# Delta-rule attention and two feed-forward networks in one kernel: attention outputs built transposed in 32-column pieces, the second network's weights staged already split, one planner for the whole order

## Chip, cores and metric

One core of a Trainium2 chip. The metric is the device time of one execution in microseconds (us), lower is better: the median of three runs. Matmuls run on PE (weights are loaded on PEld); DVE, ACT and POOL are the three elementwise engines; SP issues all DMAs.

## What is computed

The reference, cut to what matters:

```python
for t in range(S):                      # S=768, batch 4, 8 heads, head dim 48
    y[:, :, t] = einsum(q_t, state)
    v_old = einsum(state, kn_t)         # kn = normalised k
    state = state + beta_t * outer(kn_t, v_t - v_old)
x = y, heads side by side               # 3072 tokens x 384
x = elu(x @ w_in1) @ w_out1             # d_ff 2048
h = x @ w_in2                           # d_ff 2048
out = ((a0+a1*h+a2*h2+a3*h3) / (1+|b0||h|+|b1|h2+1e-6)) @ w_out2
```

The four weight matrices are float64 on the host and reach the kernel as their int64 bits; the kernel turns them into fp32 itself.

## The kernel before, in words

**Numbers.** Every product of the two networks is made of three fp32r matmuls: high part of the weight by high part of the data, high by low, low by high. A "split" (`split`, L519) makes the high part as an ACT copy that rounds to fp32r and the low part as a subtraction on DVE or POOL. The products of the attention are plain fp32 matmuls, which the trace shows as two PE records each.

**Attention.** The 768 tokens are cut into 12 scan steps `s` of 64 tokens; two steps make a window `w` (`WINS`). `g_item` (tile `gp`) makes the Gram blocks of a step, `t_pieces` solves the triangular systems of a window on DVE, and `chain` (L848) does the sequential part of each step for two halves `hf`: `ks`, `u1`, `lo`, `u2` (tiles `ks`, `cb`), `yy` (the outputs, L934), `xx` (L957) and `ku` (the update of the state `s_bd`). `yy` makes y token by feature, 64x96 at a time: 8 matmuls on the state and 8 on the step's own updates `ub`, accumulated in one PSUM tile of 128x384. An ACT copy (DVE for step 0) brings it to SBUF, `xx` transposes it with three PE transposes, a second ACT copy puts the result into `xs`, and `split_x` (L838) splits the window's `xs` into `xh` and `xl`, one buffer each.

**First network.** For each window and each of 16 feature blocks `f`: `H` (9 matmuls, tile `h`), `A1`/`B1`/`C1` (the elu and its split, tiles `e`, `pe`, `gh`, `gl`), `wo_split` (the output weights are split anew in every window), `O` (9 matmuls into the accumulators `o`). The attention of window w+1 runs between the H and O of window w. `evac1` writes a window's result to DRAM (`x2d`); its third part goes through `tmp`, the scratch tile of `t_pieces`.

**Weights.** `conv_x`, `conv_d`, `conv_s` (L603 to L633) turn a half block of float64 bits (128x192 pairs, tile `raw`) into fp32: two ACT operations, two DVE operations, and a split or a store. Windows 1 to 4 have 8 such half blocks each: the second network's output weights `o2`, stored as fp32 in `w2d`. Its input weights `i2` (32 half blocks) are converted and split in window 5, the last, where `load_w2`/`split_w2` also read `o2` back (tile `w2r`) and split it.

**Second network.** 48 steps `k` of two feature blocks each: `H2` (18 matmuls, PSUM `h_b` for even k, `h_a` for odd), `A2`/`B2`/`C2` (the rational function), `O2` (18 matmuls). `h_a` takes the PSUM of the first network's `h` tiles, so `pair_tile` waits for their last reader.

**What sets the order.** All operations are recorded (`Recorder`), each with an event time given by `at(...)`. `order` (L309) runs a list scheduler (`simulate`, costs in `PEC`, `LEAVE`, `ENTER`, `PAIR`) six times with due times from `backward`, and the best order is emitted. That holds for operations up to event time `P + Q["tm"]`; the rest, nearly all of the second network, is emitted in event order. All instructions carry the line of the recorder's call, so the trace is read by tile names.

Of the kernel before, what the change touches and what calls it, by code (L numbers as in the profile page):

```python
# [172 lines left out]
class Recorder:  # L173
    LAT = 70

# [67 lines left out]
    def act(self, out, in_, **kw):  # L243
        n = out.ids.size
        d = 200 + n * .833 - (30 if in_.base.psum else 0)
        extra = [x for x in kw.values() if isinstance(x, View)]
        d += 90 * len(extra)
        self.add("ACT", self.nc.scalar.activation, dict(out=out, in_=in_, **kw), [out], [in_] + extra, d - 100, d)
# [6 lines left out]
    class Eng:  # L255
# [3 lines left out]
        def __getattr__(self, op):  # L259
            def call(*pos, **kw):  # L260
# [26 lines left out]
                self.rec.add(self.name, fn, kw, outs, ins, d - (80 if self.name == "DVE" else 40), d, port=port)  # L287
# [11 lines left out]
    "xx": (90, 405), "wm": (200, 500)}  # L299
LEAVE = {"F": 2040, "so": 1062, "lo": 812, "ks": 804, "gp": 914, "ku": 855, "yy": 1471, "xx": 290, "wm": 500}  # L300
ENTER = {"F": 0, "so": 71, "ks": 71, "xx": -25, "ku": 70, "yy": 20, "gp": -20, "lo": 100, "wm": 50}
PAIR = {
# [3 lines left out]
FAR = 1 << 60  # L306
# [33 lines left out]
def simulate(ops, given=None):  # L340
# [3 lines left out]
    bus = 0.0  # L344
    port = 0.0
    gleft, gready = {}, {}
    mode, size, began = None, 0, 0.0
    done = 0
    rank = {}
# [6 lines left out]
    queue = None  # L356
    if given is not None:
        queue = {e: [] for e in free}
        for o in given:
            u = o.group if o.group is not None else o  # L360
            if o.group is None or o.group.ops[0] is o:
                rank[u] = len(queue[o.eng])
                queue[o.eng].append(u)
        turn = dict.fromkeys(free, 0)

    def pri(u):
        return u.n if isinstance(u, Group) else u.late

    def push(u, r):
        e = "PE" if isinstance(u, Group) else u.eng  # L370
        k = rank[u] if rank else r
        heapq.heappush(pend[e], (k, u.ops[0].n if isinstance(u, Group) else u.n, r, u))
    for o in ops:
        if o.group is None:
            if not o.left:
                push(o, 0.0)
        elif o.group.ops[0] is o and not gleft[o.group]:
            push(o.group, 0.0)
    total = sum(1 for o in ops if o.group is None) + len(gleft)
    end = 0.0  # L380

    def finish(o, t):
        nonlocal end
        end = max(end, t)
        for s in o.succ:
            k = s.deps[o]
            if s.group is not None and s.group is o.group:
                continue
            r = o.start if k == "s" else t + (0 if o.eng == "PE" else 33 if s.eng != "POOL" or s.eng == o.eng else 75)
            if s.group is not None:  # L390
                g = s.group
# [4 lines left out]
            else:  # L396
                s.ready = max(s.ready, r)
                s.left -= 1
                if not s.left:
                    push(s, s.ready)  # L400
    while done < total:
        pick = None
        for e in free:
            if queue is not None:
                if not pend[e] or pend[e][0][0] != turn[e]:
                    continue
                t = max(free[e], pend[e][0][2])
            else:
                if not pend[e] and not head[e]:
                    continue  # L410
                t = free[e]
                if not head[e]:
                    t = max(t, pend[e][0][0])
            if pick is None or t < pick[0]:
                pick = t, e
        t, e = pick
        if queue is not None:
            u = heapq.heappop(pend[e])[3]
            turn[e] += 1
        else:  # L420
            while pend[e] and pend[e][0][0] <= t:
                _, n, r, u = heapq.heappop(pend[e])
                heapq.heappush(head[e], (pri(u), n, u))
            i = 0
            if e == "PE" and mode not in (None, "F"):
                small = [x for x in head[e] if x[2].kind != "F"]
                if small:
                    i = head[e].index(min(small))
            u = head[e][i][2]
            head[e].remove(head[e][i])  # L430
            heapq.heapify(head[e])
        if e == "PE":
            if mode is not None:
                t = max(t, began + pe_cost(mode, u.kind) * size)
            mode, began = u.kind, t
            size = 1.0
            if u.kind == "F":
                size = len(u.ops) / 9
            elif u.kind == "yy":
                size = len(u.ops) / 16  # L440
# [5 lines left out]
        else:  # L446
            o = u
            o.start = t
            if e == "SP":
                free[e] = t + o.pitch  # L450
                bus = max(bus, t + 300) + o.bytes / 230.0
                finish(o, max(t + o.lat, bus + 1300) + 100)
            else:
                d = 0.0
                if o.port:
                    w = max(0.0, port - t - 135)
                    if w > 0:
                        d = w
                    port = t + d + o.lat
                free[e] = t + d + o.pitch  # L460
                finish(o, t + d + o.lat)
# [995 lines left out]
```

## Time and profile before

| | us |
|---|---|
| median of 3 runs | 1054.34 (1053.87 to 1055.9) |
| the profiled execution | 1053.65 |
| its span, first to last instruction | 1051.9 |
| PE busy | 986.0 |
| DVE busy | 886.6 |
| ACT busy | 752.4 |
| POOL busy | 429.6 |

The profiled execution's time holds 1.75 us beside its span, and lies 0.69 below the median. The program has three stretches: up to 95.6 us only attention runs (Gram blocks, the first solve, scan steps 0 and 1); from 95.6 to about 650 the first network runs with the attention of the next window between its matmuls; from about 650 the second network runs. A busy time of PE is no measure of its speed; how far apart equal blocks of matmuls start is.

### The profile page before, as it was taken

How to read it: one execution, taken by the hardware profiler on the slowest of the kernel's cores; microseconds unless marked ns; L12 is line 12 of the kernel's file. 1: busy time of each engine (PE TensorE's matmuls, PEld its weight loads, DVE VectorE, ACT ScalarE, POOL GpSimd, SP SyncE). 2: the span in 40 equal slices, each digit the busy share in tenths (PEclk: the TensorE clock that was granted, in tenths of full speed). 3: DMA queues.
4: the chain of work that ended last, by engine and by line, in shares of the span. 5: the costliest groups of instructions: out<-in, count | busy, mean ns of one | idle time of the engine just before them, and what ended most of it. 6: DMA issues, size and time to landing. Idle time of an engine off the chain costs nothing.

```text
span 1051.9 us, 22800 instructions
## 1 busy us (share of the span) xinstructions
PE 986.0 (94%) x9064; PEld 813.2 (77%) x9064; DVE 886.6 (84%) x1234; ACT 752.4 (72%) x1477; POOL 429.6 (41%) x351
## 2 busy tenths in 40 slices
PE   7159998999989999999999999999999999999997
PEld 6047876878878887888888887788888888888885
DVE  4988976987798588849943689999999999999997
ACT  4479879877677777666656999777667677676764
POOL 1376555544303222312322355554534545436332
PEclk9568989999999999999999998999999999999999
DMA  9656145514651652043020435101001010010000
GB/s 259 207 152 201 38 131 169 179 60 117 186 189 48 185 148 101 17 132 107 12 88 1 135 106 158 61 1 60 0 1 61 1 60 1 1 61 1 31 1 30
DMA packets 51852, 91.89 MB, mean 87 GB/s; under 512 B 7073, under 2 KB 29729, under 8 KB 51745
## 3 DMA queue, kind: packets, MB, share of 16 engines
q1 hardware_dynamic: 51744, 90.43, 28.1%
q8 instruction: 71, 1.16, 0.5%
q14 instruction: 37, 0.30, 0.1%
HBM read 77.83 MB, written 12.58 MB: 86 GB/s over the span
## 4 chain that ended last, share of the span: by engine, by line
PE 68%; DVE 14%; ACT 12%; issue 3%; DMA 1%; POOL 1%; SPq 0%; ACTq 0%; DVEq 0%; POOLq 0%
PE o L193 29%; PE h L193 11%; PE h_a L193 9%; PE h_b L193 8%; DVE tmp L193 3%; PE gp L193 3%; PE y L193 3%; PE cb L193 3%; ACT wo L193 2%; ACT e L193 2%; DVE wo L193 2%; PE ku L193 1%; DVE tt L193 1%; ACT raw L193 1%; DVE gl L193 1%
## 5 line engine op out<-in xcount | busy, mean ns | idle before, releaser
L193 POOL TENSOR_TENSOR gl<-wo 128x1024 fp32r<-128x1024 f32 x47 | 146.3, 3113 | 197.1 <-DVE wo L193 157.4
L193 POOL TENSOR_TENSOR wor<-wo,wor 128x384 fp32r<-128x384 f32 x96 | 113.6, 1184 | 244.3 <-ACT wor L193 221.5
L193 PE MATMUL o<-gh,wor 128*128 128x512 f32 x576 | 198.7, 404 | 7.9 <-ACT wor L193 4.3
L193 ACT ACTIVATE wo<-wo 128x192 f32<-128x192 f32 (+3 forms) x254 | 150.5, 631 | 70.5 <-DVE wo L193 62.0
L193 PE MATMUL h<-xh,wi 128*128 128x512 f32 x546 | 183.7, 396 | 1.4 <-issue 0.6
L193 PE MATMUL o<-gh,wo 128*128 128x512 f32 x576 | 139.0, 390 | 0.1
L193 PEld LDWEIGHTS o<-gh,wor 128*128 128x128 f32 x576 | 109.7, 191 | 35.4 <-ACT wor L193 5.0
L193 PEld LDWEIGHTS o<-gh,wo 128*128 128x128 f32 x576 | 107.5, 188 | 23.8 <-ACT ys L193 0.9
L193 PEld LDWEIGHTS h<-xh,wi 128*128 128x128 f32 x546 | 102.3, 188 | 25.7 <-issue 1.1
L193 PE MATMUL o<-gl,wor 128*128 128x512 f32 x288 | 114.2, 397 | 0.0
L193 DVE SCALAR_TENSOR_TENSOR e<-e,pe 128x512 f32<-128x512 f32 x96 | 78.6, 819 | 35.4 <-ACT e L193 33.3
L193 PE MATMUL h<-xl,wi 128*128 128x512 f32 x273 | 106.7, 391 | 1.2 <-DVE tt L193 0.9
L193 DVE TENSOR_TENSOR gl<-e,gh 128x512 fp32r<-128x512 f32 x88 | 70.8, 805 | 32.1 <-ACT gh L193 31.9
L193 PE MATMUL h_a<-xh,wi 128*128 128x512 f32 x288 | 93.9, 394 | 2.1 <-DVE wo L193 2.1
L193 PE MATMUL h_b<-xh,wi 128*128 128x512 f32 x288 | 93.2, 392 | 0.0
L193 DVE SCALAR_TENSOR_TENSOR wo<-wo 128x1024 f32<-128x1024 f32 (+2 forms) x71 | 81.8, 1157 | 7.4 <-ACT wo L193 7.3
L193 ACT ACTIVATE e<-h 128x512 f32<-128x512 f32 x91 | 54.1, 594 | 46.2 <-PE h L193 42.0
L193 ACT ACTIVATE gh<-e 128x512 fp32r<-128x512 f32 x96 | 60.3, 629 | 30.2 <-PE o L193 17.6
L193 PE MATMUL o<-gl,wo 128*128 128x512 f32 x288 | 73.5, 390 | 1.6 <-DVE gl L193 1.6
L193 DVE SCALAR_TENSOR_TENSOR gh<-wo,ab_sb 128x1024 fp32r<-128x1024 f32 (+1 forms) x49 | 65.9, 1344 | 6.4 <-ACT wo L193 0.2
L193 PEld LDWEIGHTS h_a<-xh,wi 128*128 128x128 f32 x288 | 54.8, 190 | 14.1 <-DVE wo L193 2.5
L193 PEld LDWEIGHTS o<-gl,wo 128*128 128x128 f32 x288 | 53.9, 188 | 13.6 <-DVE gl L193 2.4
(126 smaller groups left out, 2085.6 us busy)
## 6 DMA issues: line engine op xcount, KB each, us to landing
kv<-c_kv SPq DMA_DIRECT2D x24, 576.0 KB, 6.4
gin<-g_in SPq DMA_DIRECT2D x69, 192.0 KB, 3.7
kq<-c_kq SPq DMA_DIRECT2D x22, 512.0 KB, 4.4
raw<-w_out SPq DMA_DIRECT2D x42, 192.0 KB, 2.8
raw<-w_in SPq DMA_DIRECT2D x34, 192.0 KB, 2.4
wo<-w_in SPq DMA_DIRECT2D x30, 192.0 KB, 3.9
xr<-x2d SPq DMA_DIRECT2D x6, 768.0 KB, 5.5
out_t<-ys SPq DMA_DIRECT2D x18, 256.0 KB, 2.3
```

Of the source, the lines that this page charges most:

```text
L193: fn(**{k: v.real() if isinstance(v, View) else v for k, v in kw.items()})
```

## The change

1. **Attention outputs.** `yy` swaps the operands: the state and the updates are now the stationary side, cut into pieces of 32 columns, and q, k or p stream with 64 columns. The result stands feature by token in PSUM, in strips of 32 partitions that follow each other in turn: 24 matmuls of 32x64 on the state and 24 on the updates in place of 8 and 8 of 64x96. `xx`, both copies and `split_x` are gone; ACT writes `xh` straight from PSUM and DVE writes `xl` from PSUM and `xh`, 128x384 per half. `xh` and `xl` have two buffers.
2. **Second network's weights.** All 64 half blocks are converted in windows 1 to 4 (16 each), split by ACT and DVE into `cs`, and stored split in DRAM (`i2d`, `o2d`). In window 5 `load_i2` and `load_o2` bring 32 blocks of 393 KB to where they are used.
3. **One order.** The planner now orders everything, in 8 rounds, with other estimates (`gap`, 8 DMAs in flight, due times with the releasing engine's delay) and a choice that may hold an engine for a more urgent operation that comes soon (`choose`).
4. **Times.** `H2(0)` and `H2(1)` get events inside window 5, both in `h_b`. Half of the Gram blocks of a window get later events. The third part of `evac1` gets its own tile `xe`; `p` and `lo` have 3 buffers in place of 4.

The core of the diff:

```diff
-                y = pa.tile([128, DM], F32, tag="pa", name="y")
-                rc.brk("yy")
+                y = pa.tile([128, 3, 128], F32, tag="pa", name="y")
+                rc.brk("yt")
+                parts = [(d["kq"], s_bd)] if s > 0 else []
+                parts.append((p_d[s], d["ub"]))
+                seen = set()
+                for n, (r, l) in enumerate(parts):
+                    for bl in range(2):
+                        for i in range(4):
+                            u = 4 * bl + i
...
+                            lt = lt.rearrange("p a b -> p (a b)")
+                            for g in range(3):
+                                c, o = divmod(3 * i + g, 4)
+                                mm(out=y[32 * o:32 * o + 32, c, 64 * bl:64 * bl + 64], lhsT=lt[:, 32 * g:32 * g + 32], rhs=rhs,
+                                   start=o not in seen, stop=n == len(parts) - 1 and bl == 1 and c == 2)
+                                seen.add(o)
...
+                xh, xl = (t[:, :, c0:c0 + 128] for t in xt[w])
+                act(out=xh, in_=y, func=AF.Copy)
+                vector.tensor_tensor(out=xl, in0=y, in1=xh.bitcast(F32), op=ALU.subtract)
...
-    w2d = dr.tile([NF, 128, DM], F32, name="w2d")
+    w2d = {k: dr.tile([NF, 128, 2, DM], F32, name=f"{k}d") for k in ("i2", "o2")}
...
+            t = mp.tile([128, 2, HD], F32R, tag="cs", name="cs")
+            split(t, e, vector)
+            rc.dma(out=w2d[k][i, :, :, cs], in_=t.bitcast(F32))
...
+    def load_i2(f):
+        rc.dma(out=wi_tile(f).bitcast(F32), in_=w2d["i2"][f])
+
+    def load_o2(f):
         wo2[f] = p2p.tile([128, 2, DM], F32R, tag=f"wo2{f}", name=f"wo2{f}")
-        split(wo2[f], w2t.pop(f), vector)
+        rc.dma(out=wo2[f].bitcast(F32), in_=w2d["o2"][f])
...
-        at(Q["g1"] + Q["g1d"] * i, fn)
+        at(Q["g1"] + Q["g1d"] * i if i < 4 else i - 40, fn)
...
-            for f in range(8):
-                conv_at(T + 2 * f + .15, .5)
+            for f in range(NF):
+                conv_at(T + f + .15, .5)
...
-        for h in range(2):
-            conv_at(T + f + Q["c5"] + .4 * h, Q["c5d"])
-        at(T + f + Q["l5"], load_w2, f)
-        at(T + f + Q["l5"] + 1, split_w2, f)
+        at(T + f + 1.1, load_i2, f)
+        at(T + f + 1.2, load_o2, f)
...
+            at(T + (8.7, 14.4)[k], H2, k)
...
-    first, then = rc.ops[:cut], rc.ops[cut:]
-    _, first = order(first, 6)
+    _, first = order(rc.ops, 8)
```

Where it moves instructions. First PE at the end of the start, from the outputs of scan step 1 to the first matmul of the first network (`h`). Before:

```order
L193 MATMUL y<-s_bd,kq 64x96 x8
L193 MATMUL y<-ub,p 64x96 x8
L193 MATMUL y<-s_bd,kq 64x96 x8
L193 MATMUL y<-ub,p 64x96 x8
L193 MATMUL xt<-cm_sb,y_1071 128x128 x3
L193 MATMUL ku<-ub,kv 48x48 x32
L193 MATMUL xt<-cm_sb,y_1098 128x128 x3
L193 MATMUL gp<-gin 128x128 x4
L193 MATMUL ks<-s_bd,kq 32x48 x64
L193 MATMUL h_1262<-xh,wi_405 128x512
```

With the change:

```order
L191 MATMUL y<-kq,s_bd 32x64 x24
L191 MATMUL y<-p,ub 32x64 x24
L191 MATMUL y<-kq,s_bd 32x64 x24
L191 MATMUL y<-p,ub 32x64 x24
L191 MATMUL ku<-ub,kv 48x48 x32
L191 MATMUL h_1262<-xh,wi_355 128x512
```

The transposes are gone, and the Gram block and `ks` of step 2 now stand behind the first `h`. Earlier in the start, 16 of the Gram matmuls (`gp`) of window 1 moved from ahead of the first solve to between the outputs of step 0 and `ks` of step 1.

Second, DVE where the second network begins (the operations on `h_b` belong to `H2`; `wo_86` is scratch of the rational function, `raw` and `ce` belong to the conversion of weights). Before, at `H2(0)`:

```order
L193 TENSOR_TENSOR wo_86<-wo_86,h_b 128x1024
L193 SCALAR_TENSOR_TENSOR raw<-raw 128x192
L193 SCALAR_TENSOR_TENSOR raw_8480<-raw_8480 128x192
L193 SCALAR_TENSOR_TENSOR ce<-raw 128x192
L193 SCALAR_TENSOR_TENSOR ce<-raw_8480 128x192
L193 SCALAR_TENSOR_TENSOR wo_86<-wo_86,ab_sb,h_b 128x1024
L193 SCALAR_TENSOR_TENSOR e<-e,pe 128x512
L193 SCALAR_TENSOR_TENSOR raw<-raw 128x192
```

With the change:

```order
L191 TENSOR_TENSOR gl<-e,gh 128x512
L191 SCALAR_TENSOR_TENSOR e<-e,pe 128x512
L191 TENSOR_TENSOR wo_86<-wo_86,h_b 128x1024
L191 TENSOR_TENSOR gl<-e,gh 128x512
L191 SCALAR_TENSOR_TENSOR wo_86<-wo_86,ab_sb,h_b 128x1024
L191 SCALAR_TENSOR_TENSOR e<-e,pe 128x512
L191 SCALAR_TENSOR_TENSOR wo_86<-wo_86 128x1024
L191 TENSOR_TENSOR gl<-e,gh 128x512
```

No conversion is left there; only the elu of window 5 (`e`, `gl`) stands between the operations of `H2(0)`.

Third, SP's queue in window 5. Before:

```order
L193 DMA raw<-w_in 128x384
L193 DMA raw_8282<-w_in 128x384
L193 DMA raw<-w_in 128x384
L193 DMA w2r<-w2d 128x384
L193 DMA raw_8346<-w_in 128x384
```

With the change:

```order
L191 DMA wi_8736<-i2d 128x768
L191 DMA i2d<-cs 256x1x192
L191 DMA wi_8766<-i2d 128x768
L191 DMA wi_8793<-i2d 128x768
L191 DMA i2d<-cs 256x1x192
L191 DMA xr<-x2d 128x3x512
L191 DMA wo_8812<-o2d 128x768
```

Loads of finished weights stand where loads of raw bits stood; a load of `wi` waits for the last reader of the first network's block in the same place.

## Rows read from the trace of the kernel before

**Rows 1.** The page: busy time of each engine.

```profile
PE 986.0 (94%) x9064; PEld 813.2 (77%) x9064; DVE 886.6 (84%) x1234; ACT 752.4 (72%) x1477; POOL 429.6 (41%) x351
```

**Rows 2.** Stretches: us, busy PE, PEld, DVE, ACT, POOL, PEclk, DMA share, GB/s.

```profile
0.00:95.60 95.60, 52.13 (x1013) 45.60 (x1013) 74.03 (x169) 59.40 (x199) 43.79 (x63) 0.71 0.71 208
...
190.00:287.00 97.00, 96.16 (x1134) 79.27 (x1128) 79.84 (x139) 70.17 (x168) 41.70 (x37) 1.00 0.43 132
...
567.00:646.40 79.40, 79.40 (x354) 65.69 (x353) 59.45 (x98) 72.78 (x179) 39.41 (x41) 1.00 0.38 117
646.40:673.10 26.70, 21.99 (x73) 16.17 (x72) 25.88 (x34) 21.46 (x43) 13.33 (x12) 0.81 0.33 104
673.10:1032.60 359.50, 359.40 (x1585) 297.07 (x1584) 346.50 (x267) 251.03 (x252) 170.15 (x75) 1.00 0.06 20
1032.60:1051.90 19.30, 13.23 (x55) 9.67 (x53) 12.95 (x18) 7.26 (x12) 2.70 (x1) 0.96 0.11 41
```

**Rows 3.** Chain of waits, 696 to 712 us: start, us, what.

```profile
701.86 4.08 PE h_a L193 x18
```

**Rows 4.** Windows 1 to 4 as one stretch: all, then tile `raw` (DVE, ACT, POOL).

```profile
190.00:567.00 377.00, 370.68 (x4935) 305.95 (x4930) 291.29 (x517) 258.98 (x575) 108.49 (x98) 1.00 0.34 107
190.00:567.00 377.00, 32.51 (x70) 25.02 (x77) 2.33 (x4) 1.00 0.34 107
```

**Rows 5.** Timeline of PE where the second network begins: [idle before <-releaser].

```profile
651.12 0.79 PE L193 MATMUL o<-gh,wor 128*128 128x512 f32 x1 [2.55 <-ACT wor L193]
...
667.31 0.50 PE L193 MATMUL h_a<-xh,wi 128*128 128x512 f32 x1 [2.10 <-DVE wo L193]
```

**Rows 6.** Chain of waits, 84 to 97 us.

```profile
85.43 3.90 PE y L193 x64
...
89.81 1.57 PE ku L193 x64
...
95.62 1.60 PE h L193 x6
```

**Rows 7.** Instructions by tile: nanoseconds of one, min/median/max.

```profile
L193 ACT ACTIVATE xs<-xt x24: 467/490/493, 71.6 to 571.2; 128x384 f32<-128x384 f32 x24
L193 DVE TENSOR_TENSOR xl<-xs,xh x18: 673/684/1505, 93.5 to 574.6; 128x512 fp32r<-128x512 f32 x18
L193 DVE TENSOR_TENSOR R<-kv,ks x22: 509/544/554, 75.9 to 551.4; 128x384 f32<-128x384 f32 x22
L193 DVE SCALAR_TENSOR_TENSOR raw<-raw x35: 344/356/1461, 206.0 to 389.8; 128x192 int32<-128x192 int32 x35
L193 DVE TENSOR_TENSOR wo<-w2r,wo x16: 543/548/952, 596.6 to 665.1; 128x384 fp32r<-128x384 f32 x16
```

**Rows 8.** Timeline of PE in the start, scan step 1.

```profile
76.60 0.28 PE L193 MATMUL cb<-R,tp_t 32*32 32x48 f32 x2 [2.72 <-DVE tmp L193]
78.55 1.50 PE L193 MATMUL cb<-R,tp_t 32*32 32x48 f32 x62 [1.67 <-DVE R L193]
```

**Rows 9.** Timeline of PE, one scan step's outputs, 387 to 398 us.

```profile
387.81 0.88 PE L193 MATMUL y<-s_bd,kq 128*64 128x96 f32 x16
...
390.60 0.55 PE L193 MATMUL xt<-cm_sb,y 128*128 128x128 f32 x3
391.08 1.64 PE L193 MATMUL ku<-ub,kv 128*48 128x48 f32 x64
392.65 0.55 PE L193 MATMUL xt<-cm_sb,y 128*128 128x128 f32 x3
392.95 0.48 PE L193 MATMUL o<-gh,wor 128*128 128x512 f32 x1
...
395.10 1.05 PE L193 MATMUL gp<-gin 96*128 96x128 f32 x8
396.08 1.58 PE L193 MATMUL ks<-s_bd,kq 128*32 128x48 f32 x128
397.59 0.50 PE L193 MATMUL h<-xh,wi 128*128 128x512 f32 x1
```

**Rows 10.** Waits of PE, 95 to 646 us: total, times, longest us.

```profile
PE o L193 <- ACT tmp L193: 2.7, 2, 2.0
```

More of the change, by code (lines that the diff above doesn't have):

```diff
@@ L343, in simulate @@
     head = {e: [] for e in free}
[L344 to L349, printed above, removed]
+    bus = port = end = began = 0.0
+    mode, size, done = None, 1.0, 0
+    gleft, gready, landed = {}, {}, []
     for o in ops:
@@ L355, in simulate @@
             gready[o.group] = 0.0
[L356 to L367, printed above, removed]
-    def push(u, r):
[L370 to L380, printed above, removed]
+    def push(u, r):
+        if isinstance(u, Group):
+            heapq.heappush(pend["PE"], (r, u.n, u))
+        else:
+            heapq.heappush(pend[u.eng], (r, u.n, u))
     def finish(o, t):
@@ L400, in finish, with choose @@
                     push(s, s.ready)
+    def choose(e, t):
+        cand = sorted(head[e])
+        for late, n, u in cand[:6]:
+            stop = t + u.pitch
+            for r, _, c in pend[e]:
+                if r < stop and stop - c.late > max(0.0, r + c.pitch - late):
+                    break
+            else:
+                head[e].remove((late, n, u))
+                return u
+        return None
+    for o in ops:
+        if o.group is None:
+            if not o.left:
+                push(o, 0.0)
+        elif o.group.ops[0] is o and not gleft[o.group]:
+            push(o.group, 0.0)
+    total = sum(1 for o in ops if o.group is None) + len(gleft)
     while done < total:
@@ L403, in simulate @@
         for e in free:
[L404 to L415, printed above, removed]
-        t, e = pick
[L417 to L431, printed above, removed]
+            if pend[e] or head[e]:
+                t = free[e] if head[e] else max(free[e], pend[e][0][0])
+                if pick is None or t < pick[0]:
+                    pick = t, e
+        t, e = pick
+        while pend[e] and pend[e][0][0] <= t:
+            _, n, u = heapq.heappop(pend[e])
+            head[e].append((u.n if e == "PE" else u.late, n, u))
         if e == "PE":
+            small = [x for x in head[e] if x[2].kind != "F"] if mode not in (None, "F") else None
+            x = min(small or head[e])
+            head[e].remove(x)
+            u = x[2]
             if mode is not None:
@@ L435, in simulate @@
             mode, began = u.kind, t
[L436 to L440, printed above, removed]
+            size = len(u.ops) / SIZE[mode] if mode in SIZE else 1.0
             for o in u.ops:
@@ L580, in raw_tile @@
             return wo1[:, i].rearrange("p (n two) -> p n two", two=2).bitcast(I32)
-        if p2q is not None and n % 2:
-            return p2q.tile([128, HD, 2], I32, tag="raw2", name="raw2")
         return mp.tile([128, HD, 2], I32, tag="raw", name="raw")
@@ L1080, in evac1 @@
             else:
-                xs = tmp[:, 0:NC]
+                xs = ap1.tile([128, 512], F32, tag="xe", name="xe")[:, 0:NC]
             act(out=xs, in_=acc[w][c][:, 0:NC], func=AF.Copy)
@@ L1132, in A2 @@
         if k not in e2:
-            e2[k] = [w[:, 1024 * (2 * i + k % 2):1024 * (2 * i + k % 2) + 1024] for i in range(3)]
+            e2[k] = [w[:, 1024 * i:1024 * i + 1024] for i in (range(3, 6) if k % 2 else range(3))]
         sq, ab, u = (t[:, n] for t in e2[k])
@@ L1358 @@
     ev.sort(key=lambda x: x[:2])
-    cut = None
     for t, _, fn, a in ev:
-        if t >= P + Q["tm"] and cut is None:
-            cut = len(rc.ops)
         fn(*a)
-    first, then = rc.ops[:cut], rc.ops[cut:]
-    _, first = order(first, 6)
+    _, first = order(rc.ops, 8)
     nc.scalar.preload_act_table_set("natural_log_exp_and_others")
     with tc.manual_schedule():
-        for o in first + then:
+        for o in first:
             o.emit()
```

176 lines of the change are left out of this document (65 added, 111 removed), and 2 rows, old and new, of the table PAIR.

## Prediction

> **What bounds the kernel now.** I read the page's busy times first: PE is busy 94% of the span, DVE 84%, ACT 72% [rows 1]. That names PE and says nothing about where it loses time. So the second view is the table by stretch [rows 2], and beside it the chain of waits [rows 3] for how far apart equal blocks start.
>
> The second network is at its pace: 18 matmuls take 4.08 us, 227 ns each [rows 3], for 359.5 us without an idle PE [rows 2]. Nothing in the change makes these matmuls cheaper. In windows 1 to 4 PE is busy 370.7 of 377 us [rows 4], so time is won there by giving PE less to do, and a faster ACT or DVE wins nearly nothing. PE is slack in two places. In the start, to 95.6 us, it is busy 52 us, at a mean granted clock of 0.71, a mixture of its two levels, 1.2 and 2.4 GHz [rows 2]. Where the second network begins, 646.4 to 673.1 us, it does four blocks of 18 matmuls, which cost 4 x 4.08 = 16.3 us at full pace, in 26.7 us, at a clock of 0.81: 10.4 us lost [rows 2, 3]. DVE is busy 25.9 of these 26.7 us, and PE waits there once for the split of `wor` and once for DVE [rows 5]. DVE is late because it still converts the `i2` weights between the first operations of the second network.
>
> The sum is made against the profiled execution, 1053.65 us; the median of the runs is 0.69 us above it.
>
> **The start.** Before, the outputs of scan step 1 begin at 85.43 and take 3.90 us; the first `h` matmul comes at 95.62 [rows 6], 6.29 us after they end. In between PE does two sets of transposes, `ku`, a Gram block and `ks`. In the new order only `ku` (1.57 us) is left, and beneath it lies the new way to `xh` and `xl`: an ACT copy of 128x384 from PSUM (0.49 us, as `xs`) and a DVE subtraction that reads PSUM (0.54 us, as `R`) [rows 7]. So `h` starts 6.29 - 1.57 = 4.7 us earlier. Against that, 16 Gram matmuls move behind the first solve, ahead of step 1. Four of them take 0.98 us at full clock [rows 9], 16 take 3.9, at most 7.8 at half. They fall where PE now waits 2.72 and 1.67 us for DVE [rows 8], 4.4 us together; I take 0.7 us as not covered, bounds 0 and 3.4. What was moved behind `h` is paid there: 0.98 for the Gram block and 1.51 for `ks` [rows 9]. Together -4.7 + 0.7 + 2.5 = **-1.5 us**. DVE's solve gives up the big transpose for window 1 and gets a few conversions of 0.36 us [rows 7] more; I call that even. Bounds -5 and +3.
>
> **Outputs and transposes, 10 scan steps behind the start.** One step now: `y` 2.79 us, transposes 0.48 and 0.30 us, 3.57 us together [rows 9]. The new step has 96 matmuls of 32 output partitions and 64 columns. The nearest row is `ks`: 64 matmuls of the same kind, four strips of 32 in turn, 48 columns, in 1.51 us, 23.6 ns each [rows 9]. The unchanged price per matmul gives 2.27 us a step; by columns (64 for 48) it is 31.5 ns and 3.02 us. I take columns, because the two kinds of row agree on it: `y` has 2.79 us for 32 matmuls, 87 ns, or 0.91 ns a column in two strips, and `ks` 0.49 ns a column in four; the price goes with the columns and halves with twice the strips. 3.57 - 3.02 = 0.55 us a step, **-5.5 us**; bounds -13 (23.6 ns) and, with no gain from the four strips, +20 (58 ns, below). TensorE: Matmul & The Clock Gate of the Trainium skill (section "Wait — 56ns, not 53.3ns?") says that the start of one matmul never follows that of another by less than about 25 ns, however few columns it has. By that the 192 records of a step would take 4.8 us and this term would be +12 us; the trace disagrees, with 128 `ks` records in 1.51 us, 11.8 ns each [rows 9].
>
> **Elementwise work.** Per window the subtractions from `xs` cost DVE 3 x 0.684 us, the new ones 4 x 0.544 [rows 7]: even. ACT loses eight copies of 0.49 us a window and three roundings, and gains four. Both lie beside PE work; nothing is counted. The third part of a window's result no longer waits for the scratch tile `tmp`; the O matmuls behind it waited 2.7 us in all [rows 10]: **-2.7 us**, bounds 0 and -4.
>
> **Conversions into windows 1 to 4.** 32 more half blocks at two DVE operations each (32.5 us for 70 of them [rows 4], 0.93 a block) are 30 us; 64 splits of 128x192 on DVE at 0.36 us, as that size costs [rows 7], are 23 us (0.27 by half of `wo<-w2r`, 18 us). DVE goes from 291 to 344 us in a stretch that I expect to last 377 - 8 x 0.55 - 2.7 = 370 us: 93% busy, beside 77% now. In the second network it is 96% busy and PE does not wait [rows 2]. I count **0** and carry the doubt as a rival. ACT gains 64 conversions at 0.33 us (25.0 for 77 [rows 4]) and 64 roundings priced alike, 42 us, in 377 - 259 = 118 us of slack.
>
> **Where the second network begins.** In window 5 the raw loads, conversions and splits go, ACT's main burden there (72.8 of 79.4 us [rows 2]), and DVE has only the elu between the operations of `H2(0)`, which now comes in mid-window. What is late next is the evacuation of the accumulators before `O2(0)`; half an `H2` stands in front of it on PE to cover it. I take **-9 us** of the 10.4, bounds 0 and -10.4. The 32 loads of 393 KB are 12.6 MB; at the 208 GB/s that the start reached [rows 2] they take 60 us of a window of 80 to 90. They queue in order on SP, each `wi` load behind the last H that reads the old block, and so may hold `xr` and `wo2` loads behind them; the blocks are needed one pair per 8.16 us, later than they can come. **0**.
>
> The paced stretch and the tail (19.3 us [rows 2]) keep their work and nearly their order: 0, within 1 us.
>
> **Sum.** -1.5 - 5.5 - 2.7 - 9 = -18.7 us: 1053.65 becomes 1034.95, as a median of runs **1035.6 us**.
>
> **Rivals.**
>
> *DVE crowds windows 1 to 4.* For it: 93% is above the densest stretch of the first network now, 79.84 of 97 us, 82% [rows 2], and the triangular solve is one long chain on DVE in the same stretch. Against it: the 96% of the second network. At 91% the four windows last 378 us, 8 more: 1043.5. The gain of 18.7 us is spent when they last 370 + 18.7 = 388.6 us, that is, when DVE gets no further than 344/388.6 = 88.5%; at 82% they last 418 and the kernel takes 1083. Chance 0.15, of which 0.05 past that point.
>
> *The four strips do not overlap.* If new pieces are priced as `y` now, 87 ns for 96 columns, 58 ns for 64 [rows 9], then the 960 pieces behind the start and the 144 of steps 0 and 1 cost 26.5 ns more each than I took, 29.3 us: 1064.9, slower. The point that decides is 48 ns a piece. For it: each piece accumulates on one written before, in the same bank. Against it: `ks`. Chance 0.04.
>
> *Each record has a floor.* `ku` takes 1.57 us for 64 records, 24.5 ns each [rows 9]; if the new records cost as much, 49 ns a piece, they take 1104 x 17.5 ns = 19.3 us more: 1054.9, no change. Against it stands `ks` with 11.8 ns: 0.02. Such a floor is the rule of the Trainium skill named above.
>
> *The loss where the second network begins stays*, with another wait (accumulators, late loads) for the one removed: the change does not do there what it says. 1044.6 us, chance 0.10.
>
> **Chances and range.** The forecast as it stands has 0.69. A measurement of this kernel can tell 0.2%, 2.1 us, from no change. Faster by more than that: nearly all of the forecast and of the last rival and two thirds of the DVE case, 0.88; slower 0.08; between them 0.04. The fast end: pieces at 23.6 ns (-7.5 more), the whole 10.4 us, the other waits in windows 1 to 4 (3.6 us), 3.5 in the start: 1020. The slow end takes in the third rival and DVE down to 89%: 1050. Some 0.07 lies below and 0.09 above.
>
> **What would show it.** Right: no `xt`; 96 `y` matmuls in about 3.0 us; first `h` near 91.6; PE without a wait of over 1 us from H(5,15) to the fourth `H2`, at a clock of 1.0; windows 1 to 4 in some 370 us with DVE above 90%. Wrong: `y` steps above 4.5 us; waits of PE on `gl`, `tp_t` or `R` in windows 2 and 3; a wait on `wi` or `wo2` loads; a first `h` no earlier than 95.

## The result: slower by 0.57%, with the profile after

The changed kernel takes **1061.86 us** as a median of four runs (1057.08 to 1066.23); the kernel before, beside it, 1054.43. The ratio is 1.0057, 95% interval 1.003 to 1.0085: slower, where 1035.6 and a gain were forecast, and outside the range of 1020 to 1050. The profiled execution of the changed kernel is the fastest of its four, 1057.08 us (span 1055.3), and stands against 1053.65 (span 1051.9): 3.4 us more, where 18.7 less were forecast. The balance below is made of these two executions; the 4.8 us from this one to the median have no profile. The ratios here and below leave out a single run, one of e7 at 1076.0 us, 1.6% above the fastest of that kernel.

The page of the changed kernel, first its busy times (as [rows 1]), then from its table of DMA queues (packets, MB, share) the one that brings instructions:

```profile
PE 973.3 (92%) x10464; PEld 809.5 (77%) x10464; DVE 886.9 (84%) x1286; ACT 737.1 (70%) x1453; POOL 421.5 (40%) x319
...
q8 instruction: 82, 1.34, 0.5%
```

The same queue on the page of the kernel before:

```profile
q8 instruction: 71, 1.16, 0.5%
```

PE's busy time went down by 12.7 us, as it should, and the kernel did not get faster. PE executes 10464 matmul records and as many weight loads where it had 9064 of each, and the instruction queue moves 11 packets more. A packet is 1.34 MB / 82 = 16 KB, and 1.34 MB over 20928 instructions is 64 bytes (1.16 MB over 18128 gives the same), so a packet holds 256 of them.

The stretches of the changed kernel (us, busy PE, PEld, DVE, ACT, POOL, PEclk, DMA share, GB/s), cut where the first `h` and the fifth `H2` begin:

```profile
0.00:97.04 97.04, 47.27 (x1056) 43.14 (x1056) 69.77 (x155) 59.79 (x204) 46.74 (x67) 0.68 0.67 197
...
651.87:680.43 28.56, 28.56 (x127) 23.66 (x126) 21.14 (x19) 20.84 (x28) 13.84 (x10) 1.00 0.23 78
680.43:1035.39 354.96, 354.96 (x1567) 294.01 (x1566) 340.62 (x262) 244.61 (x244) 166.15 (x68) 1.00 0.05 18
1035.39:1055.30 19.91, 13.01 (x55) 9.80 (x53) 13.28 (x17) 7.26 (x12) 2.41 (x1) 0.97 0.10 40
```

The line from 651.87 answers to the 26.7 us at a clock of 0.81 in [rows 2]: where the second network begins PE has no idle moment now and the full clock. From the fifth `H2` to the end both kernels take the same (374.7 us before, from 677.21; 374.9 after). So the whole loss lies ahead of 651.87, as the waits of PE show. After, from the first `h` to the fifth `H2` (total, times, longest us):

```profile
PE ku L191 <- issue: 7.3, 5, 2.4
PE y L191 <- issue: 4.3, 5, 1.3
...
PE gp L191 <- issue: 1.5, 1, 1.5
PE ks L191 <- issue: 1.5, 2, 1.2
```

Before, the same stretch:

```profile
PE h L193 <- issue: 0.6, 1, 0.6
...
PE ks L193 <- issue: 0.3, 1, 0.3
```

"issue" is time in which PE waited for nothing that the profile shows: 14.6 us in place of 0.9 (16.7 and 1.7 over the whole program), all of it in or just behind `y`, `ku` and `ks`. The longest such wait, in the timeline of PE:

```profile
195.48 0.36 PE L191 MATMUL y<-p,ub 128*32 128x64 f32 x9 [0.62 <-issue]
...
197.16 0.74 PE L191 MATMUL ku<-ub,kv 128*48 128x48 f32 x22
200.30 1.71 PE L191 MATMUL ku<-ub,kv 128*48 128x48 f32 x42 [2.40 <-issue]
201.94 0.80 PE L191 MATMUL h<-xh,wi 128*128 128x512 f32 x1
```

`ku` stops after 22 of its 64 records, which have the same operands as the other 42, and goes on 2.40 us later. What happens meanwhile, by the DMA queues of 197.5 to 198.5 us (in the 4 us before, no packet of this queue starts):

```profile
q8 instruction: 1, 0.02, 5.6%
```

One packet of instructions comes in while PE stands. This is so of the other waits too. If PE's records (matmuls, weight loads and semaphores) are counted in the order of the trace, the wait above stands after 19 x 256 + 194 of them. Each of the 14 waits of this kernel, and of the 3 of the kernel before, stands after some multiple of 256 and 193 or 194 more, and so do 106 of the 107 waits on issue in all sixteen traces of this document; each ends 2.2 to 3.6 us after a packet has begun. PE comes to the end of a block of 256 instructions before the next one is there. The stretches around the wait show what follows:

```profile
197.00:199.00 2.00, 0.90 (x36) 0.68 (x24) 1.74 (x5) 1.30 (x5) 0.91 (x1) 1.00 0.92 301
199.00:201.00 2.00, 0.70 (x24) 0.70 (x26) 0.19 (x1) 0.00 (x0) 0.00 (x0) 0.93 0.23 88
201.00:203.00 2.00, 2.00 (x27) 1.72 (x24) 1.91 (x5) 0.00 (x0) 0.00 (x0) 0.50 0.57 135
```

The wait costs a second time: behind it the granted clock is 0.50, the lower level of 1.2 GHz, and the rest of `ku` takes 1.64 us for 42 records, 39 ns each instead of 24.5.

The new `y` itself is as fast as forecast. Half a step:

```profile
357.80 0.88 PE L191 MATMUL y<-kq,s_bd 128*32 128x64 f32 x48
358.50 0.85 PE L191 MATMUL y<-p,ub 128*32 128x64 f32 x48
359.28 0.93 PE L191 MATMUL ku<-ub,kv 128*48 128x48 f32 x32
```

1.48 us for 96 records, 15.4 ns each: 2.96 us a step. In the start, the first solve's arrival at PE, a wait on issue, `y` of step 1 and the first `h`:

```profile
61.49 1.90 PE L191 MATMUL cb<-kv,tp_t 32*32 32x48 f32 x64 [35.14 <-DVE tp_t L191]
...
82.74 0.36 PE L191 MATMUL ks<-s_bd,kq 128*32 128x48 f32 x11 [2.11 <-issue]
...
90.56 1.51 PE L191 MATMUL y<-kq,s_bd 128*32 128x64 f32 x48
...
97.04 0.49 PE L191 MATMUL h<-xh,wi 128*128 128x512 f32 x1
```

From the beginning of `y` to `h` it is 6.5 us instead of 10.2 [rows 6], as the change meant; but `y` begins 5.1 us later. The first solve came to PE at 57.75 us before.

**The balance of the two profiled executions**, us; blocks measured from one block's start to the next, waits taken off:

| step of the prediction | forecast | measured |
|---|---|---|
| first `h` (transposes gone, Gram blocks ahead of it) | -4.0 | +1.4 |
| Gram block and `ks` behind `h` (`gp` 31.1 before and after, `ks` 14.0 to 16.4) | +2.5 | +2.4 |
| `y` and transposes behind the start (36.8 to 30.8) | -5.5 | -6.0 |
| wait on `tmp` | -2.7 | -2.7 |
| where the second network begins | -9 | -10.4 |
| other waits of PE, from the first `h` to the fifth `H2` (7.9 to 10.4) | 0 | +2.5 |
| waits on issue in the same stretch | not in the sum | +13.7 |
| `ku` (14.3 to 16.9) | not in the sum | +2.6 |
| from the fifth `H2` on | 0 | +0.2 |
| sum | -18.7 | +3.7 (3.4 by the spans) |

### The profile page after: what moved, and what is told of

It is laid out like the page before. It is cut to its first block, busy times and chain, and to the rows that moved or that the text cites. A ratio compares the mean times of both kernels' runs of the same rounds, so it can differ in the third digit from the quotient of the medians.

```text
span 1055.3 us, 25704 instructions
## 1 busy us (share of the span) xinstructions
PE 973.3 (92%) x10464; PEld 809.5 (77%) x10464; DVE 886.9 (84%) x1286; ACT 737.1 (70%) x1453; POOL 421.5 (40%) x319
## 3 DMA queue, kind: packets, MB, share of 16 engines
q8 instruction: 82, 1.34, 0.5%
## 5 line engine op out<-in xcount | busy, mean ns | idle before, releaser
L191 POOL TENSOR_TENSOR wor<-wo,wor 128x384 fp32r<-128x384 f32 x96 | 125.8, 1311 | 256.5 <-ACT wor L191 248.6
L191 POOL TENSOR_TENSOR gl<-wo 128x1024 fp32r<-128x1024 f32 x47 | 143.5, 3054 | 198.7 <-DVE wo L191 132.4
L191 PEld LDWEIGHTS h<-xh,wi 128*128 128x128 f32 x546 | 104.5, 191 | 24.5 <-ACT xh L191 2.2
L191 DVE SCALAR_TENSOR_TENSOR e<-e,pe 128x512 f32<-128x512 f32 x96 | 75.8, 790 | 48.1 <-ACT e L191 47.5
L191 PE MATMUL h_b<-xh,wi 128*128 128x512 f32 x300 | 96.4, 389 | 0.0
L191 DVE TENSOR_TENSOR gl<-e,gh 128x512 fp32r<-128x512 f32 x88 | 73.8, 839 | 20.2 <-ACT gh L191 19.9
L191 DVE SCALAR_TENSOR_TENSOR wo<-wo 128x1024 f32<-128x1024 f32 (+2 forms) x71 | 84.3, 1189 | 7.8 <-ACT wo L191 7.6
L191 PE MATMUL h_a<-xh,wi 128*128 128x512 f32 x276 | 88.9, 389 | 0.0
L191 ACT ACTIVATE raw<-raw 128x192 f32<-128x192 f32 (+1 forms) x164 | 53.5, 376 | 20.8 <-DMA raw<-w_in 11.1
L191 ACT ACTIVATE wor<-wo 128x384 fp32r<-128x384 f32 x96 | 50.4, 525 | 21.9 <-PE o L191 19.4
L191 PEld LDWEIGHTS h_b<-xh,wi 128*128 128x128 f32 x300 | 56.3, 188 | 11.7
```

The costliest lines, as they stand in the source:

```text
L191: fn(**{k: v.real() if isinstance(v, View) else v for k, v in kw.items()})
```

## The experiments

Theory A is that PE runs out of instructions in dense runs of small matmuls. All runs in one table: time (median), ratio to the kernel before with its interval, waits of PE on issue in the whole program, when the first solve reaches PE, and the first `h` (the last three of the profiled execution, which is one of the runs: e7's is 10 us below its median, those of e4, e6 and e13 are the slowest of theirs). The runs were made in four groups (e1 to e4, e5 to e8, e9 to e12, e13 to e15), each beside runs of the kernel before, with medians of 1055.1 to 1056.7; the ratio is to those. Kernels of different groups, and the change, are best compared by their ratios: 0.001 is 1.05 us. Each kernel is ordered anew by its planner, so a difference between two holds that of their orders too; the waits on issue are followed in the traces for that reason.

| kernel | us | ratio, interval | issue | solve | first h |
|---|---|---|---|---|---|
| before | 1054.4 | | 1.7 | 57.75 | 95.6 |
| the change | 1061.9 | 1.0057, 1.003 to 1.0085 | 16.7 | 61.49 | 97.04 |
| e1_oldy | 1049.7 | 0.9964, 0.9941 to 0.9988 | 0.7 | 61.01 | 101.89 |
| e2_wide | 1096.7 | 1.0392, 1.0362 to 1.0421 | 0.2 | 60.28 | 106.92 |
| e3_spread | 1059.3 | 1.0042, 1.0016 to 1.0068 | 11.2 | 60.59 | 96.49 |
| e4_before_newy | 1073.1 | 1.0179, 1.0144 to 1.0214 | 20.2 | 58.52 | 96.33 |
| e5_sorted | 1052.6 | 0.9966, 0.9943 to 0.9988 | 2.9 | 61.05 | 97.76 |
| e6_gp | 1068.0 | 1.0122, 1.0084 to 1.016 | 15.4 | 62.56 | 99.56 |
| e7_newplan | 1069.3 | 1.0101, 1.0067 to 1.0134 | 10.8 | 60.47 | 98.18 |
| e8_ku2 | 1084.3 | 1.0279, 1.024 to 1.0318 | 9.4 | 58.40 | 100.36 |
| e9_nokq | 1049.5 | 0.9929, 0.9904 to 0.9954 | 16.6 | 60.93 | 95.88 |
| e11_oldplan | 1059.6 | 1.0034, 1.0012 to 1.0056 | 2.4 | 57.89 | 99.02 |
| e12_sorted_oldplan | 1060.6 | 1.0044, 1.002 to 1.0068 | 3.7 | 57.51 | 95.31 |
| e13_oldy_urg | 1072.8 | 1.0148, 1.012 to 1.0177 | 9.1 | 52.99 | 95.84 |
| e14_sorted_urg | 1055.6 | 1.0007, 0.9986 to 1.0029 | 4.3 | 52.18 | 88.77 |
| e15_after_urg | 1062.4 | 1.0062, 1.0038 to 1.0086 | 15.7 | 52.92 | 88.43 |

### The old y in the changed kernel, and the new y alone

> The changed kernel with the outputs computed as before: y token by feature, 16 matmuls of 64x96 a half, one SBUF copy (one buffer), three transposes; xh and xl are still made straight from the PSUM of the transposes; staged weights, planner and times of the change stay. Theory A (supply): PE runs out of instructions because the new y has three times as many. Then the waits of PE put down to issue fall from 16.7 us to under 3, y with transposes goes back from 30.8 to about 37 us behind the start, the first h comes some 4 us later, and the time is near 1055 us (1051 to 1059). Theory B (load): the issue waits come from the staged weights, 109 MB of DMA instead of 90, whatever y looks like. Then they stay above 8 us and the time is 1066 us or more.

```diff
-                y = pa.tile([128, 3, 128], F32, tag="pa", name="y")
-                rc.brk("yt")
+                y = pa.tile([128, DM], F32, tag="pa", name="y")
+                rc.brk("yy")
...
+                    rc.transpose(ps[:, c], d["y1"][:, 128 * c:128 * c + 128], id_sb)
...
-                act(out=xh, in_=y, func=AF.Copy)
+                act(out=xh, in_=ps, func=AF.Copy)
```

1049.7 us, 0.36% faster than the kernel before. Its waits of PE on `ub` and on issue:

```profile
PE y L191 <- ACT ub L191: 5.4, 4, 2.6
...
PE ks L191 <- issue: 0.7, 1, 0.7
```

All but 0.7 us of the waits on issue are gone, with the staged weights, their DMA and the planner in place: theory A, not B. The first `h` comes even later, at 101.89, and the kernel is faster all the same, somewhat more so than A had said (1051 to 1059).

> The kernel before with one part of the change alone: y in 32-column pieces, transposed, no transposes; ACT writes xs from PSUM and the split of xs stays; weights, planner, times and loads are those of before. Theory A (supply): issue waits of 8 us or more appear at the old volume of DMA (90 MB); y with transposes saves about 6 us, and the time is 1055 to 1062 us. Theory B (load): issue waits stay near 2 us and the time is about 1047 us (1044 to 1050), the saving that was forecast for y and the start.

```diff
-                rc.brk("yy")
+                rc.brk("yt")
...
+                act(out=box["xs"][:, :, c0:c0 + 128], in_=y, func=AF.Copy)
...
-                (sl[6] + Q["xo"], mk((xx, 0))), (sl[8] + Q["xo"], mk((xx, 1)))]
```

The waits of PE, whole program:

```profile
PE ku L193 <- issue: 8.7, 4, 3.3
PE ks L193 <- issue: 7.9, 3, 4.5
...
PE y L193 <- issue: 3.6, 5, 1.1
```

20.2 us of waits on issue come with the new `y` alone, at the old volume of DMA; 1073.1 us, slower than either theory said. In both kernels, then, the new `y` costs time: by the ratios 10 us in the change, 19 in the kernel before.

### Fewer instructions in y

> The changed kernel with the same outputs, transposed, but in 8 pieces of 64 or 32 columns per four blocks instead of 12 of 32: 64 matmuls a step instead of 96, the same work in each strip of columns. Theory A (supply): a step's y brings 256 PE instructions instead of 384, so the issue waits fall from 16.7 to 3 to 8 us and the time to about 1052 us (1048 to 1056), y itself staying near 3 us a step. Theory B (load): issue waits stay at 14 to 19 us and the time within 3 us of 1061.9. A third possibility, that 64-wide pieces do not overlap in the strips, would show as y above 4 us a step.

```diff
-                            for g in range(3):
-                                c, o = divmod(3 * i + g, 4)
...
+                            for a, z in ((0, 64), (64, 96)) if i % 4 in (0, 2) else ((0, 32), (32, 96)):
+                                c, o = divmod(96 * i + a, 128)
...
```

The waits on issue vanish, but for another reason: `y` now takes 8.0 us a step, as the timeline of one shows from its first row to the `ku` behind it.

```profile
207.11 2.27 PE L191 MATMUL y<-kq,s_bd 128*64 128x64 f32 x31
...
215.12 0.29 PE L191 MATMUL ku<-ub,kv 128*48 128x48 f32 x2
```

That is 125 ns a piece of either width in this mixed order (64, 32, 32, 64); sorted, they take 68 and 36 (next run). So slow a `y` says nothing on supply; behind the start it takes 80.0 us instead of 30.8. The next run sorts the same pieces by width.

> The same pieces of 64 and 32 columns as in e2_wide, 64 matmuls a step, but all pieces of 64 columns of a half first, then all of 32, so that neighbours in PE's queue have one width except at one place. In e2_wide a step of y took 8.0 us, 125 ns a piece, with widths in turn. If it is the change of width that keeps pieces from overlapping, a step now takes 2.8 to 3.3 us; then theory A (supply) expects issue waits of PE under 6 us in all and a time of 1046 to 1054 us. If pieces of 64 columns do not overlap at all, a step takes 5 us or more and the time is above 1070.

```diff
+                wide = [(64, i, a, 64) for i, a in ((0, 0), (2, 0), (1, 32), (3, 32))]
+                slim = [(32, i, a, 32) for i, a in ((0, 64), (1, 0), (2, 64), (3, 0))]
+                todo = [(n, bl, p) for ps in (wide, slim) for n in range(len(parts)) for bl in range(2) for p in ps]
...
```

Half a step:

```profile
163.70 0.69 PE L191 MATMUL y<-kq,s_bd 128*64 128x64 f32 x16 [1.83 <-ACT ub L191]
...
164.79 0.43 PE L191 MATMUL y<-kq,s_bd 128*32 128x64 f32 x16
...
165.37 0.92 PE L191 MATMUL ku<-ub,kv 128*48 128x48 f32 x32
```

1.67 us a half, 3.3 a step: sorted, the pieces overlap. Waits on issue 2.9 us, time 1052.6, as theory A expected. `y` is somewhat slower than in the change and has two thirds of its instructions, and the kernel is 9.3 us faster (9.6 by the ratios).

### The same instructions, spread

> The changed kernel with one more rule in the planner: after more than 40 small matmuls (y, ku, ks, cb) the next PE group is a block of H or O if one is ready within 2 us. Not one instruction more or less; in five of the eleven steps the two halves of y now stand apart, with blocks of 9 large matmuls between them, in the others y still stands as 96 in a row. Theory A (supply): the waits on issue vanish in the steps that are spread and stay in the others; 5 to 10 us in all, time 1053 to 1058. Theory B (load): issue waits unchanged at 14 to 19 us, time within 3 us of 1061.9.

```diff
+            big = [x for x in head[e] if x[2].kind == "F"] if dense > 40 else None
...
-            x = min(small or head[e])
+            x = min(big or small or head[e])
...
+            dense = 0 if u.kind == "F" else dense + len(u.ops) if u.kind != "gp" else dense
```

A step that the rule spread (between 263.7 and 266.06 a block of nine large matmuls runs), then one that it could not:

```profile
262.32 0.88 PE L191 MATMUL y<-kq,s_bd 128*32 128x64 f32 x48
263.02 0.85 PE L191 MATMUL y<-p,ub 128*32 128x64 f32 x48
...
266.06 0.92 PE L191 MATMUL ku<-ub,kv 128*48 128x48 f32 x32
266.92 0.88 PE L191 MATMUL y<-kq,s_bd 128*32 128x64 f32 x48
...
401.09 0.48 PE L191 MATMUL y<-kq,s_bd 128*32 128x64 f32 x19 [1.34 <-issue]
...
404.77 0.33 PE L191 MATMUL ku<-ub,kv 128*48 128x48 f32 x5 [0.99 <-issue]
```

This is the cleanest of the runs: in the five spread steps there is not one wait on issue (in the change, each of them had at least one), and all eight that are left stand in the start and in the steps that stayed dense. What was won there went into other waits (`cb` on `R` 5.6 us, `h` on `wi` 2.6). The waits on issue, 11.2 us in all, and the time, 1059.3, lie just above what A had said, and the time is still within what B had said; by the intervals the time is not told apart from the change, so this run shows where the waits come from and not what they cost.

### More instructions without a new y, and less DMA

> The kernel before with the state update ku in two matmuls of 24 columns where there was one of 48: twice the PE instructions of ku (256 instead of 128 a step and half, not one column more), everything else as before. Theory A (supply): the number of instructions alone makes PE run dry; issue waits, 1.7 us in the kernel before, come to 5 to 15 us in all, in ku or in what stands behind it, and the time to 1059 to 1070. Theory B (the new y's form or the load of the staged weights): issue waits stay below 3 us and the time within 3 us of 1054.4.

```diff
-                        mm(out=ps[64 * h:64 * h + D, u], ... rhs=d["ub"][:, u, h], start=True, stop=True)
+                        for q in (slice(0, 24), slice(24, 48)):
+                            mm(out=ps[64 * h:64 * h + D, u, q], ... rhs=d["ub"][:, u, h, q], start=True, stop=True)
```

The waits of PE, whole program:

```profile
PE ks L193 <- issue: 6.4, 5, 2.3
...
PE xt L193 <- issue: 2.4, 1, 2.4
```

9.4 us of waits on issue in the kernel before, by instructions alone. The time, 1084.3, is above what theory A said, because the halved matmuls cost as much as whole ones: `ku` takes 29.1 us instead of 14.3 behind the start. From 409.99 to 412.98 126 of its records with 24 columns take 23.7 ns each, beside 24.5 with 48 [rows 6]. So the time cannot be put down to the waits alone.

> The changed kernel without the loads of kq from scan step 2 on (it leaves out 20 loads of 512 KB and goes on with the kq of step 1), every PE instruction as in the change. The longest issue waits stand where the DMA engines are 89 to 104% busy, because the end of y and ku frees the buffers of kq and kv and sets off their loads. Theory A2 (PE's next instructions come late because their transfer shares the DMA engines with these loads): the issue waits fall from 16.7 us to under 8 and the time to 1050 to 1057. Theory A1 (the density of instructions is enough by itself): issue waits stay at 12 to 19 us, time 1058 to 1064.

```diff
+            if nm == "kq" and s > 1:
+                t = kq_k[hf]
...
```

The waits of PE, whole program:

```profile
PE ku L191 <- issue: 6.7, 5, 2.3
PE y L191 <- issue: 5.6, 6, 1.5
...
PE ks L191 <- issue: 3.2, 2, 1.7
```

The waits on issue stay, 16.6 us: the density of instructions is enough (A1), and these loads do not make them. The time fell by 12.4 us (13 by the ratios) nevertheless, to just below what A2 had said, though the waits exclude its reason. In the profiled executions `h` comes 1.2 us earlier and the stretch to the fifth `H2` is 6.7 us shorter; what in the loads of `kq` costs that was not settled.

### The start and the planner

> The changed kernel with the Gram blocks of window 1 back at their old times, all eight ahead of the first solve; for that p and lo have four buffers again, the third part of a window's result goes through the scratch tile tmp again, and cs has one buffer. Theory C (Gram blocks): they delay the start; then the first h comes at 92 to 94 us instead of 97.0 and the time is 1056 to 1060. Theory D (planner): the new rules put more conversions between the steps of the first solve; then the first triangular solve still reaches PE at 60.5 us or later (57.75 before, 61.49 with the change), the first h comes at 95 to 98, and the time stays within 3 us of 1061.9. Issue waits stay at 12 to 19 us in both.

```diff
-        at(Q["g1"] + Q["g1d"] * i if i < 4 else i - 40, fn)
+        at(Q["g1"] + Q["g1d"] * i, fn)
...
```

> The kernel before with the new planner alone (its costs, due times, holding rule, 8 rounds), for the same part of the program as before; y, weights, event times and buffers are those of before. Theory D (planner): the first solve reaches PE at 60 to 62 us instead of 57.75, the first h at 98 to 101 instead of 95.6, time 1055 to 1061. Theory C (Gram blocks): 57 to 58.5, first h at 94 to 96.5, time 1050 to 1056. Issue waits below 3 us in both.

The edit of e7 replaces the kernel's `Recorder`, `order`, `simulate` and `backward` by those of the change. The first solve at PE in e7, then a wait on issue:

```profile
60.47 0.78 PE L191 MATMUL cb<-kv,tp_t 32*32 32x48 f32 x18 [30.11 <-ACT wi L191]
...
403.58 0.27 PE L191 MATMUL ks<-s_bd,kq 128*32 128x48 f32 x2 [3.98 <-issue]
```

For the start theory D holds: with the Gram blocks back the solve comes no earlier than in the change (62.56, 61.49 there), and with the new planner alone it comes at 60.47. By the column of the table it reaches PE at 57.5 to 58.5 in every kernel with the old planner and at 60.3 to 62.6 in every one with the new, whatever else is in them (e13 to e15, with one more rule, aside). As a whole e6 is slower than either theory said, 1068.0 us and a first `h` at 99.56; which of its edits costs that was not settled. And e7 costs more than D said, 11 us by the ratio, and has 10.8 us of waits on issue with the old `y`, where both theories had less than 3: here the planner put `y`, transposes, `ku`, a Gram block and `ks` in a row, 540 instructions without a large matmul.

> e1_oldy (the change with the old y) with the planner of the kernel before, for the same part of the program as there: of the change only the staged weights, the times of H2, the late Gram blocks and the direct xh and xl are left. Theory E (the new planner costs time by itself, in the start and by bunching small matmuls): first h at 95 to 98 us instead of 101.9, time 1042 to 1048. Theory F (the staged weights need the planner, which carries the gain where the second network begins): time 1050 to 1058, with waits of PE between 640 and 680 us.

> e5_sorted (the change with 64 pieces of two widths, sorted) with the planner of the kernel before, for the same part of the program as there. Theory E: first h at 92 to 96 us instead of 97.8, issue waits under 6 us, time 1043 to 1049. Theory F: time 1051 us or more, with waits of PE between 640 and 680 us.

Both put the old planner, with its cut, into e1_oldy and e5_sorted. Both theories fail: the kernels are slower by 9.9 and 8.0 us (1059.6, 1060.6; 7 and 8 by the ratios), though no wait of PE of over 0.6 us stands between 640 and 680. The first solve is early, as E said:

```profile
57.89 0.34 PE L193 MATMUL cb<-kv,tp_t 32*32 32x48 f32 x2 [36.11 <-ACT wo L193]
```

What is lost lies in the windows (in e11 waits of PE on `tp_t`, 7.0 us, and on `gh` and `gl`, 5.7). With the staged weights and e1's or e5's `y` the new planner is worth 7 to 10 us; with the weights of before it costs 11.

> The changed kernel with one more rule in the planner: the operations of the first triangular solve (window 0) are the most urgent on their engine, so that no conversion of weights stands between its steps on DVE. In ten kernels the first solve reached PE at 57.5 to 58.5 us with the old planner and at 60.3 to 62.6 with the new one. Theory G (conversions between the steps of the solve are what the new planner costs in the start): the solve reaches PE at 54 to 58 us instead of 61.5, the first h comes at 90 to 94 instead of 97.0, issue waits stay at 14 to 19 us, time 1055 to 1059. Theory H (the work put aside is needed for the first h anyway): the solve is earlier, but the first h comes at 96 us or later or waits on wi follow, time 1060 to 1065.

```diff
-        o.late = late
+        o.late = late - (1e6 if o.urg else 0)
...
```

The first solve and the first `h`:

```profile
52.92 0.34 PE L191 MATMUL cb<-kv,tp_t 32*32 32x48 f32 x2 [26.65 <-DVE tp_t L191]
...
88.43 0.50 PE L191 MATMUL h<-xh,wi 128*128 128x512 f32 x1
```

The waits of PE from there to 190 us:

```profile
PE o L191 <- ACT wor L191: 4.3, 3, 2.4
PE h L191 <- ACT wi L191: 2.4, 2, 1.8
PE o L191 <- POOL wor L191: 2.1, 5, 0.7
```

Conversions between the steps of the solve are indeed what delays it (G), by 8.6 us, more than G had said: between its first and its last operation DVE does 10 of them in the kernel before (3.9 us), 15 in the change (8.4 us) and 2 here (0.7 us). But the first `h`, 8.6 us earlier, buys nothing (H): in window 0 PE waits for the weights whose conversion was put aside, and the kernel takes 1062.4 us, as without the rule.

> e1_oldy (the change with the old y, 1049.7 us) with the same rule. Theory G: first h at 95 to 98 us instead of 101.9, time 1044 to 1047. Theory H: first h at 101 us or later or waits on wi, time 1048 to 1053.

> e5_sorted (the change with 64 pieces of two widths, sorted, 1052.6 us) with the same rule. Theory G: first h at 91 to 95 us instead of 97.8, issue waits below 6 us, time 1047 to 1050. Theory H: first h at 97 us or later or waits on wi, time 1051 to 1056.

1072.8 and 1055.6 us: `h` is 6 and 9 us earlier and both kernels are slower than without the rule. In e13 9.1 us of waits on issue came back with the old `y`, in two waits of `ks`; by the ratios it is 19 us slower than e1, and the rest of that was not followed.

The fastest kernels that keep the whole computation are e1_oldy and e5_sorted, alike by their ratios (0.9964 and 0.9966): the change with the old `y`, and with fewer instructions in the new one.

## Why the prediction was wrong

- **The price of a piece was right.** "31.5 ns and 3.02 us" a step: measured 2.96, and -6.0 us for the ten steps. Neither the four strips nor a floor was the matter: 15.4 ns a record, below the 24.5 of the third rival.
- **What failed** is a term that the sum put at nothing, behind the step "I take columns": it priced the new matmuls by columns alone and had no term for bringing 192 matmul records and 192 weight loads a step to PE, where there had been 64 and 64. Waits on issue were in the trace of before (1.7 us) and were not priced. They came to +13.7 us behind the first `h` and 2.1 in the start (0.8 before), and `ku` and `ks` are slower around them. Where the waits stand, at the ends of blocks of 256 instructions, and e1, e3, e4 and e8 show it: same change without the instructions, same instructions spread, instructions alone, other instructions.
- In numbers of this trace: half a step of `y` is 192 instructions in 1.48 us, 7.7 ns each, and `ks` 256 in 1.51, 5.9 ns; the old `y` took 2.79 us for 128, 21.8 ns [rows 9]. Two halves with their `ku` are 512, two packets. The Trainium skill, Runtime: NRT & Kernel Launch, section "Instruction fetch mechanics", says that instructions come in blocks of 256 and that crossing into the next block is mostly hidden. The packets agree with the first. On the second the trace agrees for most crossings and not for the dense runs: PE waits at 14 of the 82 blocks of the change, up to 2.40 us, and at 3 of the 71 of the kernel before.
- **The start.** "DVE's solve gives up the big transpose for window 1 and gets a few conversions of 0.36 us [rows 7] more; I call that even." Not even: the solve reaches PE 3.7 us later; it starts 1.4 us later, and conversions between its steps take 4.6 us more of DVE (2.2 more in e7, with the new planner alone; e15 takes nearly all of them out). This is the second step that failed: the first `h` came at +1.4 us where -4.0 was forecast. The step behind it was wrong in kind: a first `h` that comes earlier was counted as time won, and e15 gets it 7 us ahead of the kernel before without winning any, while e1 is 6 us behind it and faster. What the conversions have done by then decides, with `h`.
- **Where the second network begins** and the wait on `tmp` went as forecast or better: -10.4 of 10.4 and -2.7.
- **DVE in windows 1 to 4** did not reach the 93% on which the first rival stood. One row of the changed kernel, the stretch of [rows 4]:

```profile
190.00:567.00 377.00, 361.62 (x5747) 300.84 (x5751) 312.37 (x624) 264.44 (x629) 114.40 (x94) 0.99 0.44 137
```

  83% for DVE. 312.4 us there instead of 344, in part because only 54 of the 64 splits lie in this stretch (24.0 us; the last begins at 601.3) and DVE's elu operation `e` takes 46.0 us where it had 51.5. It cost nothing: PE waits 2.0 us for `gl` in all between the first `h` and the fifth `H2`.

- **The range.** "The slow end takes in the third rival and DVE down to 89%: 1050" does not follow: the third rival was priced at 1054.9, and DVE at 89% gives 344 / 0.89 = 386.5 us, 16.5 more than 370 and so 1052. The 0.2% that a measurement was to tell was too fine as well: the interval of the result is 0.55% wide.

What stays open: what sets the moment at which a packet of instructions starts. In e7 `ks` waits 1.63 us on issue at 301.27, behind the same run of `y`, transposes, `ku`, a block of O and a Gram block that passes in the kernel before without a wait [rows 9]. In both a block of 256 ends at a record of `ks`; in the kernel before the packet for the next one began 7.3 us earlier, in e7 2.5. Density decides that PE can run dry; when the packet starts, with it, decides whether it does. Open are also the 12.4 us of e9.

## What to carry to other kernels

Price a burst of small matmuls twice, by columns and by the instructions it takes (here four per fp32 matmul): 512 in a row without a large matmul, at 6 to 12 ns each, ran dry in most steps of the change; runs of 192 or 256 between blocks of nine large ones did not in the spread steps of e3. That is no safe bound: `ks` alone, 256 behind a Gram block, ran dry in e7. Before cutting a matmul into pieces that overlap better, look for waits on issue in the trace and for what stands behind the burst. In this kernel a first `h` that came earlier was worth nothing by itself (e15): a block that starts earlier is worth something only if what its successors need is earlier too: ask what was put aside for it.

## What the runs showed of the hardware

- Waits of PE on issue stand at the ends of blocks of 256 of its instructions (106 of 107 waits in sixteen traces, at 193 or 194 records beyond a multiple of 256) and end 2.2 to 3.6 us after a packet of 16 KB has begun.
- Behind the wait of 2.40 us on issue at 200.30 the granted clock of 201 to 203 us was 0.50, and `ku` took 39 ns a record instead of 24.5.
- Pieces of 64 and 32 columns in mixed order cost 125 ns each (e2), all of one width in a row 68 ns (64) and 36 ns (32), by e5's rows: 1.09 us for 16 of the one, 0.58 for 16 of the other.
- In `ku`, whose matmuls alternate between two halves of the output, a record takes 23.7 ns with 24 columns (e8) and 24.5 with 48; in four strips `y` needs 15.4 with 64. The rule of "Wait — 56ns, not 53.3ns?" (TensorE: Matmul & The Clock Gate, the Trainium skill), a floor near 25 ns, comes near the first two and does not fit the third.
